# Two 64-column tiles for the last keys' product with V, and a plan with hand-over times per pair of engines

## The chip, the cores and the metric

The kernel runs on one core of one Trainium2 chip. The metric is device time in microseconds (us) of one execution. The engines are PE (TensorE, matrix products), DVE (VectorE), ACT (ScalarE), POOL (GpSimd) and SP, whose queue issues every DMA.

## What is computed

Three stages, one after the other, on 8 batches of 576 rows:

```python
scores = scale * np.matmul(q, k.transpose(0, 1, 3, 2))      # 8 heads, head_dim 64
thresh = np.max(scores, axis=-1, keepdims=True) - tau
scores = np.where(scores >= thresh, scores, -1000000000.0)
attn = softmax(scores); x = attn @ v                        # heads side by side: 512 columns
k = np.maximum(xk @ w_k, 0.0)     # xk, xr mix a row with the one before it
v = k * k @ w_v                   # 512 -> 1024 -> 512
x = sigmoid(xr @ w_r) * v
gate = sigmoid(conv(x))           # causal convolution over rows, 5 taps for each column
out = (gate * (x @ w_val)) @ w_out
```

All inputs are float32 (the weights float64). Attention's product with V is done in fp32. The scores and the five weight products are done as sums of three fp32r products of split operands: high with high, high with low, low with high.

## The kernel before, in words

Attention goes over 32 pairs of heads. A pair is cut into 9 chunks of 128 query rows by 576 keys: four for one head, four for the other, and a last one that holds the 64 left-over rows of both. For each chunk PE makes the scores (L524; L534 for the first pair), DVE takes the minimum (L549), ACT the exponential (L562), POOL adds the threshold (L552), DVE masks and sums (L571), POOL normalizes (L584). Then the probabilities are turned on PE: in the first four pairs straight from `p` in fp32 (L610), after that from a copy `pr` that a DMA makes (L638), in fp32r (L608). ACT brings the result back (L621, L624; the last 64 keys in L629, L632).

Twice a pair follows the product with V, once for 256 columns of query rows and once for 320. The two heads write the two halves of one PSUM bank: for each of four groups of 128 keys, L674 multiplies V of one head into partitions 0 to 63 and V of the other into 64 to 127, each as a column tile of 128 rows by 64 columns of the array. The last 64 keys of both heads come in one product over all 128 rows and 128 columns (L677): `v[:, 512:640]` holds V of head one in its upper left quarter, V of head two in its lower right quarter and zeros elsewhere. As operands are fp32, each product is two matmul instructions in the trace: 16 of L674 and 2 of L677 for each of the 64 products with V.

The first gated layer (names `xk`, `k`, `kh`, `vo`; products with `w_k` and `w_v` at L751) runs in blocks of 512 rows and is woven into the attention of later batches, since a block needs whole rows of x. The tail, after attention, holds the last products with `w_v` and then, block by block, the products with `w_r` (`r`), `w_val` (`val`) and `w_out` (`out`), 36 of each, 12 matmuls a product, all at L751. Between them DVE mixes rows for r (L810), multiplies y = gate times v (L1023), does the convolution's four later taps (L1067, in place in PSUM, two instructions a tap where a block spans two batches) and multiplies gate with val (L1090).

The order of everything is set at build time. Each step is an `Op` with an engine, a duration, what it waits for, a priority and the buffers that it takes and gives back. `Plan.order` is a list scheduler: it plays the program through with these durations and lets each free engine take the ready step of lowest priority number. What it finds is the fixed order of instructions on each engine; on the chip an engine then waits for semaphores in that order. Some steps may go to either of two engines (the low halves on DVE or POOL, the squares on ACT or POOL), and the plan decides. Of waits it knew one number: a step that depends on another engine is ready `HOP` ns after the other ends, a DMA's reader `DMA_MARGIN` later still:

```python
push(end + hop, "free", pick)
x.ready = max(x.ready, end + pick.lat + (DMA_MARGIN if e == "dma" else 0.0) + (SAME.get(e, 0.0) if x.eng == e else hop))
```

The keys (`EARLY`, `W_KEY`, `MIX2`, `CONV_LAG`, `OUT_LAG` and others) shift the priorities of kinds of steps against each other.

Of the kernel before, what the change touches and what calls it, by code (L numbers as in the profile page):

```python
# [63 lines left out]

class Op:
    __slots__ = ("eng", "dur", "lat", "fn", "prio", "acq", "rel", "after", "left", "ready", "start", "idx", "got",
                 "port", "mode")


class Plan:  # L70
# [7 lines left out]
        self.ops = []  # L78
        self.tokens = {}

    def op(self, eng, dur, fn, deps=(), prio=0.0, acq=(), rel=(), lat=0.0, port=False, mode=0):
        o = Op()
        o.port, o.mode = port, mode
        o.eng, o.dur, o.lat, o.fn, o.prio, o.acq, o.rel = eng, dur, lat, fn, prio, acq, rel
        o.start = None
        o.after, o.ready, o.idx = [], 0.0, len(self.ops)
        o.left, o.got = 0, []
        for d in deps:
            if d is not None:
                d.after.append(o)  # L90
                o.left += 1
        self.ops.append(o)
        return o

    def order(self, hop):


        free = dict(self.tokens)
        since = {}
# [3 lines left out]
        n = 0  # L103
        port, mode = 0.0, 0
# [13 lines left out]
        while events:  # L118
            now = events[0][0]
            while events and events[0][0] <= now:  # L120
                _, _, kind, o = heapq.heappop(events)
# [7 lines left out]
                            since[x] = now  # L129
            for e in ENGINES:  # L130
                while busy[e] <= now and ready[e]:
                    skipped, pick, held = [], None, None
                    while ready[e]:
                        x = heapq.heappop(ready[e])
                        if x[2].start is not None:
                            continue
                        if held is not None and x[0] > held[0] + PORT_SLACK:
                            skipped.append(x)
                            break
                        if all(any(free[a] > 0 for a in t) if isinstance(t, tuple) else free[t] > 0  # L140
                               for t in x[2].acq):
                            if e == "dve" and x[2].port and port > now + PORT_TOL:
                                if held is None:
                                    held = x
                                    continue
                            else:
                                pick = x[2]
                                break
                        skipped.append(x)
                    if held is not None:  # L150
                        if pick is None:
                            pick = held[2]
                        else:
                            skipped.append(held)
                    if e == "pe" and mode == 1 and pick is not None and pick.mode != 1:
                        late = pick.prio + GANG
                        while ready[e]:
                            x = heapq.heappop(ready[e])
                            if x[2].mode == 1 and x[0] <= late and all(free[t] > 0 for t in x[2].acq):
# [9 lines left out]
                        break  # L169
                    for t in pick.acq:  # L170
                        if isinstance(t, tuple):
                            t = min((a for a in t if free[a] > 0), key=lambda a: since.get(a, 0.0))
# [7 lines left out]
                    if e == "pool" or e == "dve" and pick.port:  # L180
                        hold = pick.dur
# [21 lines left out]
                    end = now + pick.dur  # L203
                    busy[e] = end
                    push(end, "idle", pick)
                    push(end + hop, "free", pick)
                    for x in pick.after:
                        x.ready = max(x.ready, end + pick.lat + (DMA_MARGIN if e == "dma" else 0.0) + (SAME.get(e, 0.0) if x.eng == e else hop))
                        x.left -= 1
                        if not x.left:  # L210
                            push(x.ready, "ready", x)
# [2 lines left out]

EARLY, QK_EARLY, T_LATE, EV_EARLY, AV_LATE = 166.8448, 0.7689, -0.6136, 186.5584, 0.3905
S3_CHUNKS = 40
MOE_LAG = 0.5912
MOE_STEP = 0.8255  # L220
KSTAGE = 3

LATE_PAIRS = 6
# [5 lines left out]
CVB = 3  # L229
GATES = {"a": 1, "b": 3}  # L230
XRS = {"a": 1, "b": 1}
MIX_EARLY, SIDE_EARLY = -36.7205, 2.0832
W_KEY, W_STEP = -0.8604, 71.1806
V_KEY, V_STEP = 38.9587, 2.2987
EXP_EARLY, MASK_EARLY, SUM_EARLY, NORM_EARLY, MOVE_EARLY, PREP_EARLY, XE_EARLY, KH_EARLY, KL_EARLY = -3.4426, 0.0367, 0.3513, 0.4532, 3.8756, 0.7807, 10.363, 1.0147, -4.2659
MORE_KEYS = ("EXP_EARLY", "MASK_EARLY", "SUM_EARLY", "NORM_EARLY", "MOVE_EARLY", "PREP_EARLY", "XE_EARLY", "KH_EARLY", "KL_EARLY")
R_AHEAD = 0
HOP, DMA_MARGIN, MARGIN = 269.8939, 482.1964, 1.011
VAL_LAG, OUT_LAG = 1.6991, 2.9796
LATE2, LOAD2, MIX2, CONV_LAG, THR_EARLY = 79.2985, -22.1186, -62.0727, 28409.2718, 280.5553  # L240
MIX_AT = 12.996
OUT_FETCH = 1039.5206

PORT_TOL, PORT_SLACK = 839.1264, 3.4377
WARM = 3400.0
SWITCH = 200.0
GANG = 5.9257
# [4 lines left out]
ENGINES = ("dma", "pe", "dve", "act", "pool", "none")  # L252


@with_exitstack
def body(ctx, tc, qka, qkb, vp, w_k, w_v, w_r, w_val, w_out, conv_w, par, out):
# [243 lines left out]
    def chunk(g):  # L500
# [163 lines left out]
        if c in (3, 8):  # L664
# [3 lines left out]
            def av():  # L668
                pt, ptl = pt_t[pi, half]
                v = v_t[pi]  # L670
                acc = av_t[pi, half] = bank(av_op[pi, half])
                for kc in range(4):
                    for h in range(2):
                        nc.tensor.matmul(acc[h * 64:h * 64 + 64, 0:n],  # L674
                                         lhsT=v[:, kc * 128 + h * 64:kc * 128 + h * 64 + 64],
                                         rhs=pt[:, h, kc, 0:n], start=(kc == 0), stop=False)
                nc.tensor.matmul(acc[:, 0:n], lhsT=v[:, 512:640], rhs=ptl[:, 0:n], start=False, stop=True)  # L677

            def evac_x():
                if half == 0:  # L680
# [181 lines left out]
    def moe1(n, at):  # L862
# [32 lines left out]
            l = f["lo"] = op(K_LO, 0, lo, (h,), pr - KL_EARLY, rel=("k2",), port=True)  # L895
            kparts.append((h, l))
        if n < NM - 1:
            mix_k(n + 1, at + MIX_AT * u)
# [284 lines left out]
```

## Time and profile before

| what | value |
|---|---|
| median of 3 runs | 1214.2 us (1214.2 to 1215.7) |
| span of the profiled execution | 1214.2 us |
| PE busy | 1181.0 us (97%) |
| DVE busy | 881.2 us (73%) |
| ACT busy | 859.7 us (71%) |
| POOL busy | 718.5 us (59%) |
| mean granted clock of TensorE | 0.998 |

The profiled execution took as long as the median, so no step between the two is needed. PE's busy time counts overlapping matmuls once, and it counts time in which an instruction has begun but its weights are not in place; a stretch that reads as 100% busy can still hold dead time. Where this matters, the distance from one instruction's start to the next is the better number.

### The profile page before, as it was taken

The page shows a single profiled execution, that of the slowest core. Times are in us where ns is not written, and L with a number is a line of the kernel's source. Part 1 is how long each engine was busy: PE and PEld are TensorE (multiplying, and loading weights), DVE is VectorE, ACT ScalarE, POOL GpSimd, SP SyncE. Part 2 cuts the span into 40 slices and gives each one's busy share as a digit, 9 for nine tenths or more (in the row PEclk, how much of TensorE's full clock was granted, in tenths as well). Part 3 has the DMA queues.
Part 4 walks back from the last instruction along what each step waited for, and adds up shares of the span by engine and source line. Part 5 has one row for each costly group of instructions (what it writes and reads, how often), then busy time and mean ns, then how long its engine had stood idle before and what let it go on. Part 6 is the DMA issues. An engine that isn't in the chain of part 4 may idle for free.

```text
span 1214.2 us, 20512 instructions
## 1 busy us (share of the span) xinstructions
PE 1181.0 (97%) x6798; PEld 948.9 (78%) x6798; DVE 881.2 (73%) x1998; ACT 859.7 (71%) x1637; POOL 718.5 (59%) x960
## 2 busy tenths in 40 slices
PE   6888999999999999999999999999999999999998
PEld 4666788878888778878788778878887877888887
DVE  7999988888888788888877767732314997666650
ACT  7998977898788678778868857745536677654432
POOL 5887776688668668667765766531205755444321
PEclk9999999999999999999999999999999999999999
DMA  6445655567655675556555455325204333221111
GB/s 224 148 160 191 220 189 216 204 234 282 228 183 199 228 243 208 191 209 228 218 209 210 171 186 182 148 86 192 70 23 186 120 124 105 94 82 59 61 52 70
DMA packets 70777, 201.38 MB, mean 166 GB/s; under 512 B 8720, under 2 KB 21136, under 8 KB 68752
## 3 DMA queue, kind: packets, MB, share of 16 engines
q1 hardware_dynamic: 70672, 200.08, 45.9%
q8 instruction: 54, 0.88, 0.3%
q14 instruction: 51, 0.42, 0.1%
HBM read 91.07 MB, written 34.67 MB: 104 GB/s over the span
## 4 chain that ended last, share of the span: by engine, by line
PE 75%; DVE 7%; DMA 3%; POOL 2%; issue 2%; ACT 1%; SPq 0%; DVEq 0%; POOLq 0%; ACTq 0%
PE g L751 47%; PE s L524 11%; PE g L674 8%; PE g L608 6%; DVE g L1067 3%; PE g L677 3%; DMA pr<-p 2%; DVE y L1023 1%; DVE xf L810 1%; DMA stage<-in_w_val 1%; DVE gate L1090 1%; DMA raw<-in_qka 1%; DVE sm L549 0%; ACT p L562 0%; POOL xrl L832 0%
## 5 line engine op out<-in xcount | busy, mean ns | idle before, releaser
L549 DVE TENSOR_REDUCE sm<-s 128x1 f32<-128x576 f32 x288 | 214.3, 751 | 71.9 <-PE s L524 63.9
L571 DVE SCALAR_TENSOR_TENSOR p<-s,sm,p 128x576 f32<-128x576 f32 x288 | 231.2, 812 | 42.0 <-ACT p L562 22.0
L562 ACT ACTIVATE p<-s,sm 128x576 f32<-128x576 f32 x288 | 212.4, 749 | 43.2 <-DVE sm L549 23.5
L584 POOL TENSOR_SCALAR p<-p,sm 128x576 f32<-128x576 f32 x234 | 188.4, 809 | 81.5 <-DVE sm L581 68.6
L524 PE MATMUL s<-qkh 128*128 128x288 f32 x620 | 194.7, 330 | 5.2 <-DVE p L571 5.0
L524 PE MATMUL s<-kl,qkh 128*128 128x288 f32 x620 | 173.6, 296 | 1.2 <-DVE kl L462 1.2
L621 ACT ACTIVATE pt<-g 128x512 f32<-128x512 f32 x256 | 145.4, 603 | 33.6 <-PE g L608 31.2
L552 POOL TENSOR_SCALAR sm<-sm,gs 128x1 f32<-128x1 f32 x288 | 109.2, 381 | 87.0 <-DVE sm L549 62.9
L674 PE MATMUL g<-pt,v 128*64 128x320 f32 (+1 forms) x1024 | 138.8, 413 | 0.9 <-ACT pt L624 0.8
L524 PEld LDWEIGHTS s<-qkh 128*128 128x128 f32 x620 | 116.8, 188 | 17.2 <-DVE p L571 4.9
L608 PEld LDWEIGHTS g<-ident_r,pr 128*128 128x128 f32 (+1 forms) x1148 | 118.9, 140 | 14.5 <-ACT p L562 2.0
L608 PE MATMUL g<-ident_r,pr 128*128 128x128 f32 (+1 forms) x1148 | 123.4, 242 | 5.9 <-ACT p L562 1.4
L1067 DVE SCALAR_TENSOR_TENSOR g<-y,cw_t,g 128x128 f32<-128x128 f32 (+25 forms) x256 | 125.0, 517 | 4.2
L524 PEld LDWEIGHTS s<-kl,qkh 128*128 128x128 f32 x620 | 117.2, 189 | 8.4 <-DVE kl L462 1.4
L751 PE MATMUL g<-xkh,w_k_hi 128*128 128x512 f32 x288 | 116.4, 404 | 0.1
L751 PE MATMUL g<-kh,w_v_hi 128*128 128x512 f32 x288 | 115.5, 401 | 0.0
L751 PE MATMUL g<-xkh,w_k_lo 128*128 128x512 f32 x288 | 112.8, 392 | 0.0
L751 PE MATMUL g<-kh,w_v_lo 128*128 128x512 f32 x288 | 112.6, 391 | 0.0
L674 PEld LDWEIGHTS g<-pt,v 128*64 128x64 f32 x1024 | 68.1, 137 | 55.7 <-issue 9.3
L468 POOL TENSOR_TENSOR qkh<-raw,qkh 64x576 fp32r<-64x576 f32 x62 | 90.1, 1454 | 15.7 <-ACT qkh L458 7.0
L832 POOL TENSOR_TENSOR xrl<-xf,xrh 128x512 fp32r<-128x512 f32 x36 | 48.3, 1351 | 76.2 <-ACT xrh L829 76.0
L1032 POOL TENSOR_TENSOR yl<-y,yh 128x512 fp32r<-128x512 f32 x36 | 48.5, 1358 | 74.6 <-ACT yh L1029 74.6
(112 smaller groups left out, 2561.4 us busy)
## 6 DMA issues: line engine op xcount, KB each, us to landing
pr<-p SPq DMA_DIRECT2D x112, 576.0 KB, 3.5
raw<-in_qkb SPq DMA_DIRECT2D x31, 640.0 KB, 4.5
raw<-in_qka SPq DMA_DIRECT2D x31, 608.0 KB, 4.6
v<-in_vp SPq DMA_DIRECT2D x32, 320.0 KB, 3.3
x_d<-x SPq DMA_DIRECT2D x32, 290.0 KB, 4.1
v_d<-vo SPq DMA_DIRECT2D x36, 256.0 KB, 2.5
vt<-v_d SPq DMA_DIRECT2D x9, 1024.0 KB, 4.8
pr<-p SPq DMA_DIRECT2D x28, 288.0 KB, 2.8
```

The source lines that it names most:

```text
L468: nc.gpsimd.tensor_tensor(out=t["hi"][lo_rows, qs], in0=t["raw"][lo_rows, qs], in1=t["hi"][lo_rows, qs].bitcast(F32), op=ALU.subtract)
L524: nc.tensor.matmul(s_t[g][:, hh, 0:NT], lhsT=q, rhs=k, start=(i == 0), stop=(i == len(terms) - 1))
L549: nc.vector.tensor_reduce(out=sm[:, 0:1], in_=s_t[g][:, :, 0:NT], op=ALU.min, axis=AX.XY)
L552: nc.gpsimd.tensor_scalar(out=sm_t[g][:, 1:2], in0=sm_t[g][:, 0:1], scalar1=tau_t, scalar2=1.0, op0=ALU.add, op1=ALU.mult)
L562: nc.scalar.activation(out=view(), in_=s_t[g][:, :, 0:NT], func=AF.Exp, bias=sm_t[g][:, 0:1], scale=-1.0)
L571: nc.vector.scalar_tensor_tensor(out=view(), in0=s_t[g][:, :, 0:NT], scalar=sm[:, 1:2], in1=view(), op0=ALU.is_le, op1=ALU.mult, accum_out=to)
L584: nc.gpsimd.tensor_scalar(out=view(), in0=view(), scalar1=sm_t[g][:, 3:4], scalar2=1.0, op0=ALU.mult, op1=ALU.mult)
L608: nc.tensor.transpose(o_.bitcast(F32R), in_=i_.bitcast(F32R), identity=ident_r)
L621: nc.scalar.activation(out=pt[:, head, :, q0:q0 + 128], in_=ps.rearrange("p (k q) -> p k q", k=4), func=AF.Copy)
L674: nc.tensor.matmul(acc[h * 64:h * 64 + 64, 0:n], lhsT=v[:, kc * 128 + h * 64:kc * 128 + h * 64 + 64], rhs=pt[:, h, kc, 0:n], start=(kc == ...
L751: nc.tensor.matmul(ps()[:, 0:tw], lhsT=W[w][wt][:, kc, m * 128:(m + 1) * 128].bitcast(F32R), rhs=a(at, kc), start=(i == 0 and x == 0), sto ...
L1067: nc.vector.scalar_tensor_tensor(out=f["ps"][:, x:at + w], in0=t["y"][:, c, x + k:at + w + k], scalar=cw[:, c, k:k + 1], in1=f["ps"][:, x: ...
```

## The change

The product of the last keys with V is cut into the same two column tiles as the other four groups of keys. The two zero quarters of `v[:, 512:640]` are still multiplied.

```diff
-                nc.tensor.matmul(acc[:, 0:n], lhsT=v[:, 512:640], rhs=ptl[:, 0:n], start=False, stop=True)
+                for h in (0, 64):
+                    nc.tensor.matmul(acc[h:h + 64, 0:n], lhsT=v[:, 512 + h:576 + h], rhs=ptl[:, 0:n], start=False, stop=True)
-            o = av_op[pi, half] = op("pe", (3000 if half else 2430) * slow, av, deps, lt + AV_LATE, acq=(BANKS,),
+            o = av_op[pi, half] = op("pe", 2930 if half else 2390, av, deps, lt + AV_LATE, acq=(BANKS,),
```

The plan's single hand-over time becomes a table by pair of engines, with a time of its own for giving back a buffer, and a factor on two durations goes:

```diff
+        def reach(e, f, hop):
+            if isinstance(f, dict):
+                return hop + max(HOPS[e][g] for g in f)
+            return SAME.get(e, 0.0) if e == f else hop + HOPS[e][f]
-                    push(end + hop, "free", pick)
+                    push(end + hop + FREE[e], "free", pick)
-                        x.ready = max(x.ready, end + pick.lat + (DMA_MARGIN if e == "dma" else 0.0) + (SAME.get(e, 0.0) if x.eng == e else hop))
+                        x.ready = max(x.ready, end + pick.lat + (DMA_MARGIN if e == "dma" else 0.0) + reach(e, x.eng, hop))
-HOP, DMA_MARGIN, MARGIN = 269.8939, 482.1964, 1.011
+HOP, DMA_MARGIN, MARGIN = 30.0, 480.0, 1.011
+HOPS = {"pe": dict(pe=0, act=200, dve=200, pool=200, dma=200, none=200),
+        "dve": dict(pe=170, act=110, dve=130, pool=175, dma=150, none=170),
...
+FREE = dict(pe=200, dve=170, act=200, pool=120, dma=100, none=0)
-        slow = 1.02
+        slow = 1.0
```

All keys of the plan get other values, of which two lines stand here for all. An operand `hold` is also added, which can keep a buffer for a step that waits; no step sets it.

```diff
-LATE2, LOAD2, MIX2, CONV_LAG, THR_EARLY = 79.2985, -22.1186, -62.0727, 28409.2718, 280.5553
+LATE2, LOAD2, MIX2, CONV_LAG, THR_EARLY = 42.4429, -35.4801, -230.8294, 12594.8319, 251.622
```

With that the order on every engine is another one. In PE's order, one product with V of 320 columns (the twentieth of the 64) stood like this before; `s` are scores, `g` a bank of PSUM:

```order
L524 MATMUL s<-qkh 128x288
L524 MATMUL s<-kl,qkh 128x288
L674 MATMUL g_3242<-pt,v 64x320 x8
L677 MATMUL g_3242<-ptl,v 128x320
L524 MATMUL s<-qkh 128x288
L524 MATMUL s<-kl,qkh 128x288
```

Now its counterpart is:

```order
L539 MATMUL s<-qkh 128x288
L539 MATMUL s<-kl,qkh 128x288
L689 MATMUL g_3278<-pt,v 64x320 x8
L693 MATMUL g_3278<-ptl,v 64x320 x2
L539 MATMUL s<-qkh 128x288
L539 MATMUL s<-kl,qkh 128x288
```

The full-width product of the last keys has become two half-width ones; the neighbours are of the same kind. The first full-width instruction behind the eight column tiles is now one of fp32r scores.

In the tail, DVE's order before went on like this after the eighth product of gate and val (`xf` is the mix for r, the rows with `cw_t` are taps):

```order
L1090 TENSOR_TENSOR gate<-g_11751,gate 128x512
L1023 TENSOR_TENSOR y<-gate,vt 128x512
L810 SCALAR_TENSOR_TENSOR xf<-xt,par_t,g_11886 128x256
L1023 TENSOR_TENSOR y<-gate,vt 128x512
L810 SCALAR_TENSOR_TENSOR xf<-xt,par_t,g_11886 128x256
L1067 SCALAR_TENSOR_TENSOR g_11798<-y,cw_t,g_11798 128x128
L1067 SCALAR_TENSOR_TENSOR g_11798<-y,cw_t,g_11798 128x380
L1067 SCALAR_TENSOR_TENSOR g_11865<-y,cw_t,g_11865 128x128
```

Now, at the same place:

```order
L1106 TENSOR_TENSOR gate<-g_11952,gate 128x512
L826 SCALAR_TENSOR_TENSOR xf<-xt,par_t,g_11977 128x192
L1039 TENSOR_TENSOR y<-gate,vt 128x512
L826 SCALAR_TENSOR_TENSOR xf<-xt,par_t,g_12004 128x320
L1039 TENSOR_TENSOR y<-gate,vt 128x512
L826 SCALAR_TENSOR_TENSOR xf<-xt,par_t,g_12004 128x192
L1039 TENSOR_TENSOR y<-gate,vt 128x512
L1083 SCALAR_TENSOR_TENSOR g_11904<-y,cw_t,g_11904 128x128
```

The mixes for later blocks' r have moved forward. Between the eighth and the ninth product of gate and val DVE now has 43 instructions (11 mixes, 4 of y, 28 taps), where it had 28 (4, 4 and 20). On PE, 19 products with `w_r` and 8 with `w_val` now stand ahead of the first with `w_out`, where it was 12 and 8; after that a round of four each goes three `r`, one `out`, one `r`, two `out`, one `val`, one `out`, three `val`, where before `out` and `r` alternated one by one and four `val` followed.

## Rows read from the trace of the kernel before

**Rows 1.** The page's head: span, and busy time of each engine.
```profile
span 1214.2 us, 20512 instructions
PE 1181.0 (97%) x6798; PEld 948.9 (78%) x6798; DVE 881.2 (73%) x1998; ACT 859.7 (71%) x1637; POOL 718.5 (59%) x960
```
**Rows 2.** Engines by stretch: length, then busy us (instructions) of PE, PEld, DVE, ACT, POOL.
```profile
0.00:20.00 20.00, 12.31 (x58) 6.74 (x60) 11.96 (x27) 13.32 (x26) 8.71 (x20) 1.00 0.73 257
60.00:105.00 45.00, 38.68 (x264) 28.40 (x262) 42.73 (x84) 40.98 (x82) 38.94 (x56) 0.96 0.51 178
150.00:300.00 150.00, 150.00 (x987) 121.59 (x987) 125.10 (x323) 122.04 (x239) 113.41 (x167) 1.00 0.61 223
920.00:1020.00 100.00, 97.37 (x424) 78.69 (x423) 91.55 (x177) 72.83 (x140) 66.52 (x53) 1.00 0.39 138
```
**Rows 3.** PE's waits from 150 to 820: total us, times, longest.
```profile
PE g L608 <- DMA pr<-p: 1.2, 1, 1.2
PE g L608 <- ACT vo L907: 1.1, 1, 1.1
PE g L608 <- ACT x L684: 0.9, 1, 0.9
PE s L524 <- DVE p L571: 0.8, 2, 0.5
```
**Rows 4.** Chain of work around two products with V: start, us, what.
```profile
245.07 2.30 PE g L674 x16
247.38 0.74 PE g L677 x2
...
257.49 1.88 PE g L674 x16
259.37 0.63 PE g L677 x2
```
**Rows 5.** PE in order of time around the same: start, us, line, tile, count.
```profile
257.20 0.29 PE L524 MATMUL s<-kl,qkh 128*128 128x288 f32 x1
257.42 1.95 PE L674 MATMUL g<-pt,v 128*64 128x256 f32 x16
259.30 0.70 PE L677 MATMUL g<-ptl,v 128*128 128x256 f32 x2
...
260.07 0.39 PE L751 MATMUL g<-xkh,w_k_lo 128*128 128x512 f32 x1
```
**Rows 6.** Chain: thirteen fp32r transposes of 128 columns in a row.
```profile
624.68 1.08 PE g L608 x13
```
**Rows 7.** PE's instructions by line, 150 to 820: the last keys' product.
```profile
L677 PE MATMUL g<-ptl,v 128*128 128x256 f32 (+1 forms) x104 | 39.1, 458 | 0.0
```
**Rows 8.** ACT by line, 20 to 110: two rows, the shortest and longest kinds used.
```profile
L454 ACT ACTIVATE qkh<-raw,gs 128x640 fp32r<-128x640 f32 (+1 forms) x9 | 7.5, 831 | 0.0
L684 ACT ACTIVATE x<-g 128x256 f32<-128x256 f32 (+1 forms) x9 | 3.9, 429 | 0.2 <-PE g L677 0.2
```
**Rows 9.** Two lines by themselves: durations min/median/max ns, first and last start.
```profile
L1023 DVE TENSOR_TENSOR y<-gate,vt x36: 682/691/1792, 922.4 to 1156.3; 128x512 f32<-128x512 f32 x36
L751 PE MATMUL g<-kl,w_v_hi x288: 387/389/475, 168.0 to 913.8; 128*128 128x512 f32 x144
```
**Rows 10.** DVE by line, 922.3 to 1022.1: busy us, mean ns, idle before.
```profile
L1067 DVE SCALAR_TENSOR_TENSOR g<-y,cw_t,g 128x128 f32<-128x128 f32 (+7 forms) x112 | 55.5, 521 | 1.7
L1023 DVE TENSOR_TENSOR y<-gate,vt 128x512 f32<-128x512 f32 x18 | 19.1, 1077 | 0.8 <-PE g L751 0.8
L810 DVE SCALAR_TENSOR_TENSOR xf<-xt,par_t,g 128x192 f32<-128x192 f32 (+4 forms) x36 | 17.0, 474 | 5.6 <-ACT g L799 4.2 <-POOL xrl L832 1.4
L1090 DVE TENSOR_TENSOR gate<-g,gate 128x512 f32<-128x512 f32 x12 | 8.1, 682 | 0.0
```
**Rows 11.** The chain's end.
```profile
1022.02 187.99 PE g L751 x828
...
1210.04 0.60 ACT o L1115
```
**Rows 12.** Chain: two of the copies that transposes waited for.
```profile
410.87 5.41 DMA pr<-p
...
711.19 7.54 DMA pr<-p
```
**Rows 13.** The page's DMA issues: KB each, median us from issue to landing.
```profile
pr<-p SPq DMA_DIRECT2D x112, 576.0 KB, 3.5
```

More of the change, by code (lines that the diff above doesn't have):

```diff
@@ L66 @@
     __slots__ = ("eng", "dur", "lat", "fn", "prio", "acq", "rel", "after", "left", "ready", "start", "idx", "got",
-                 "port", "mode")
+                 "port", "mode", "hold")
 class Plan:
@@ L79, in __init__, with op @@
         self.tokens = {}
-    def op(self, eng, dur, fn, deps=(), prio=0.0, acq=(), rel=(), lat=0.0, port=False, mode=0):
+    def op(self, eng, dur, fn, deps=(), prio=0.0, acq=(), rel=(), lat=0.0, port=False, mode=0, hold=()):
         o = Op()
-        o.port, o.mode = port, mode
+        o.port, o.mode, o.hold = port, mode, hold
         o.eng, o.dur, o.lat, o.fn, o.prio, o.acq, o.rel = eng, dur, lat, fn, prio, acq, rel
@@ L131, in order @@
                 while busy[e] <= now and ready[e]:
-                    skipped, pick, held = [], None, None
+                    skipped, pick, held, kept = [], None, None, ()
                     while ready[e]:
@@ L139, in order @@
                             break
-                        if all(any(free[a] > 0 for a in t) if isinstance(t, tuple) else free[t] > 0
-                               for t in x[2].acq):
+                        if all(any(free[a] > 0 and a not in kept for a in t) if isinstance(t, tuple)
+                               else free[t] > 0 and t not in kept for t in x[2].acq):
                             if e == "dve" and x[2].port and port > now + PORT_TOL:
@@ L148, in order @@
                                 break
+                        elif x[2].hold and free["x"] > 0:
+                            kept = x[2].hold
                         skipped.append(x)
@@ L158, in order @@
                             x = heapq.heappop(ready[e])
-                            if x[2].mode == 1 and x[0] <= late and all(free[t] > 0 for t in x[2].acq):
+                            if x[2].mode == 1 and x[0] <= late and all(free[t] > 0 and t not in kept for t in x[2].acq):
                                 skipped.append((pick.prio, pick.idx, pick))
@@ L171, in order @@
                         if isinstance(t, tuple):
-                            t = min((a for a in t if free[a] > 0), key=lambda a: since.get(a, 0.0))
+                            t = min((a for a in t if free[a] > 0 and a not in kept), key=lambda a: since.get(a, 0.0))
                             pick.got.append(t)
@@ L213, in order @@
         return out
-EARLY, QK_EARLY, T_LATE, EV_EARLY, AV_LATE = 166.8448, 0.7689, -0.6136, 186.5584, 0.3905
+EARLY, QK_EARLY, T_LATE, EV_EARLY, AV_LATE = 75.1647, 1.8278, -2.0346, 153.7854, 1.5185
 S3_CHUNKS = 40
 MOE_LAG = 0.5912
-MOE_STEP = 0.8255
+MOE_STEP = 0.7879
 KSTAGE = 3
@@ L231 @@
 XRS = {"a": 1, "b": 1}
[L232 to L235, printed above, removed]
+MIX_EARLY, SIDE_EARLY = -34.628, 2.644
+W_KEY, W_STEP = -1.5423, 25.8964
+V_KEY, V_STEP = 20.9718, 6.154
+EXP_EARLY, MASK_EARLY, SUM_EARLY, NORM_EARLY, MOVE_EARLY, PREP_EARLY, XE_EARLY, KH_EARLY, KL_EARLY = -2.5135, 0.0304, 0.3776, 0.5121, 2.3441, 2.7971, 2.9697, 1.433, 0.072
 MORE_KEYS = ("EXP_EARLY", "MASK_EARLY", "SUM_EARLY", "NORM_EARLY", "MOVE_EARLY", "PREP_EARLY", "XE_EARLY", "KH_EARLY", "KL_EARLY")
 R_AHEAD = 0
-HOP, DMA_MARGIN, MARGIN = 269.8939, 482.1964, 1.011
-VAL_LAG, OUT_LAG = 1.6991, 2.9796
-LATE2, LOAD2, MIX2, CONV_LAG, THR_EARLY = 79.2985, -22.1186, -62.0727, 28409.2718, 280.5553
-MIX_AT = 12.996
-OUT_FETCH = 1039.5206
-PORT_TOL, PORT_SLACK = 839.1264, 3.4377
+HOP, DMA_MARGIN, MARGIN = 30.0, 480.0, 1.011
+VAL_LAG, OUT_LAG = 2.4158, 4.2372
+LATE2, LOAD2, MIX2, CONV_LAG, THR_EARLY = 42.4429, -35.4801, -230.8294, 12594.8319, 251.622
+MIX_AT = 1.1188
+OUT_FETCH = 1042.669
+PORT_TOL, PORT_SLACK = 842.0121, 3.4087
 WARM = 3400.0
 SWITCH = 200.0
-GANG = 5.9257
+GANG = 2.2937
 RAW_TO = 1
@@ L252 @@
 ENGINES = ("dma", "pe", "dve", "act", "pool", "none")
+HOPS = {"pe": dict(pe=0, act=200, dve=200, pool=200, dma=200, none=200),
+        "dve": dict(pe=170, act=110, dve=130, pool=175, dma=150, none=170),
+        "act": dict(pe=200, act=0, dve=195, pool=185, dma=150, none=200),
+        "pool": dict(pe=120, act=60, dve=50, pool=0, dma=100, none=120),
+        "dma": dict(pe=0, act=0, dve=0, pool=0, dma=0, none=0),
+        "none": dict(pe=0, act=0, dve=0, pool=0, dma=0, none=0)}
+FREE = dict(pe=200, dve=170, act=200, pool=120, dma=100, none=0)
 @with_exitstack
@@ L897, in moe1 @@
         if n < NM - 1:
-            mix_k(n + 1, at + MIX_AT * u)
+            mix_k(n + 1, at + MIX_AT)
         for m in range(KD):
```

## Prediction

> **What bounds the kernel now.** I read the page's head first: PE is busy 97% of the span, the other engines 59 to 73% [rows 1]. The stretches show where the missing time sits. From 150 to 300 us PE has no idle time at all [rows 2], and from 150 to 820 its named waits come to 4.0 us in five waits, none over 1.2 us [rows 3]. Before 150 us it is different: in 60 to 105 us PE lacks 6.3 of 45 us while DVE is busy 42.7 and ACT 41.0 [rows 2]; the softmax and the splitting of weights set the pace there. In the tail PE lacks 2.6 us between 920 and 1020 while DVE is busy 91.6 of 100 [rows 2], and DVE's own rows between 922.3 and 1022.1 add up to 99.7 us of work in 99.8 us [rows 10]. After 1022.0 the chain is 828 matmuls of `L751` without a break, 188.0 us or 0.227 us each, then one eviction at 1210.0 [rows 11]. So the end is set by PE's work, plus what PE loses in the first 150 us, plus what it loses until DVE lets go at 1022.
>
> **The product of the last keys.** 64 more columns make sixteen column-tile matmuls 2.30 instead of 1.88 us long [rows 4]. They run in eight pairs, so a pair costs 0.42/8 = 0.0525 us per 64 columns, 0.21 us for 256. Eight pairs are 1.68 of 1.88 us: 0.20 us is not columns. The two full-width matmuls take 0.63 us for 256 columns and 0.74 for 320 [rows 4], of which 2 x 0.21 and 2 x 0.2625 are columns: 0.21 us is dead, in both. The order in time splits the dead time [rows 5]. The last score starts at 257.20, needs 0.13 and is followed at 257.42: 0.09 us. From 259.30, the first of `L677`, to 260.07, the second of `L751`, are 0.77 us, of which 0.42 and 0.227 are columns: 0.12 us, the wait for the first 128 fp32 weights. The rest of the 0.21, again about 0.09, lies before `L677` starts. Each change between the half and the full width thus costs about 0.09, and the fp32 weights behind it 0.12.
>
> After the change the last keys are one more round like the four before: four matmuls in two pairs, 2 x 0.21 us, as much as the two full-width ones took in columns. The change of width is still there, but now the instruction behind it is an fp32r one. Thirteen fp32r transposes in a row take 1.08 us, 0.083 each [rows 6]; 128 columns in one pass are 0.21/4 = 0.053, so a load of 128 fp32r weights shows at most 0.03 us. The saving is 0.12 - 0.03 = 0.09 us a product if 0.09 for the width stays. Its ends are 0 (all dead time moves to the next instruction) and 0.21 (all goes). Of the 128 `L677` matmuls 104 stand where PE is never short of work [rows 7], so 52 of the 64 products count: 52 x 0.09 = 4.7 us, ends 0 and 10.9. I take 4.7, by the transposes, the nearest full-width fp32r rows.
>
> Two rules of the Trainium skill bear on this. "TensorE: Matmul & The Clock Gate", section "Weight-path perf modes", has 128 weights that are not FP32 load faster than FP32 ones; rows 6 against the 0.12 us of rows 5 agree, and the sum by it is the one above. "TensorEngine Tiling (Array Packing)", section "Key Properties", says that changing the tiling mode drains TensorE; the 0.09 us on both sides of rows 5 agree, and by that rule alone nothing is saved, since the change of mode only moves behind the new pairs.
>
> **The start.** Counted in the order, ten ACT instructions fewer stand ahead of the first product with `w_k` (two exponentials, two casts of keys and queries, pieces of weights and others). At 0.43 to 0.83 us each [rows 8] that is about 6.7 us. But at the 84th matmul of that layer the instructions ahead of it on ACT are again as many: 158.8 us of work now, 159.3 before, each kind at its mean duration. The head start is spent before PE has stopped waiting for ACT, and I count 0, with ends of -6.7 (it is all kept) and +2 (the same work with two more waits of the size of rows 3).
>
> **The middle.** All of it is moved, and none of PE's work is added or taken but that of the first part. PE idles 4.0 us there [rows 3]; the ends are -4.0 and +4.0, and I take 0, since PE's queue of ready work is what covers the moves. Without that cover each late copy would cost about 1.2 us [rows 3].
>
> **The tail.** PE's work behind the last product with `w_v` (913.8 us, rows 9) is the same: 1284 matmuls, 291.5 us. What differs is how much DVE must have done ahead of a given place. Before, the binding place is 456 matmuls in: DVE starts y at 922.4 [rows 9] and gives the last of 18 y, 36 mixes, 112 taps and 12 gate products at 1022.0; 828 matmuls remain, 188.0 us. Now the worst place by the order is 661 matmuls in, behind 27 y, 50 mixes, 176 taps and 16 gate products. With rows 10 (0.496 a tap, 0.472 a mix, 0.675 a gate product, 19.1 for the first 18 y) and the median 0.691 for 9 further y [rows 9] that is 87.3 + 23.6 + 10.8 + 25.3 = 147.0 us: DVE is there at 1069.4, 623 matmuls or 141.4 us remain, and PE ends at 1210.8, where it was 1210.0. If the 8.1 us of idle time in rows 10 does not recur in the added work, the 47.3 added us shrink by the same share to 43.5, PE ends at 1207.0 by this place, and DVE is no longer what ends last. With every y at the 1.06 us of the first 18, it would be 3.3 later. So -3.0 to +4.1; I take 0, between the two nearest results.
>
> **Sum.** 1214.2 - 4.7 + 0 + 0 + 0 = 1209.5 us, against a span and a median that are both 1214.2.
>
> **The rivals.**
> *The width's price only moves (no change).* The exit from half width, weights included, costs the next instruction the same 0.21 us. For it: the price of the width is there on both sides in rows 5, and rows 6 show fp32r weights only where the width does not change. Against it: the 0.12 us of rows 5 belong to fp32 weights. Then the sum is 1214.2, with +-2 from the new order. By the skill's rule on draining this is the result.
> *More is saved.* Both parts of the 0.21 us go, for instance because the next weights are in place by then: 52 x 0.21 = 10.9, hence 1203.3. Nothing in the rows shows weights of the full width loaded under column tiles.
> *DVE binds later in the tail (slower).* Moving the mixes for r forward puts 43 instead of 28 DVE instructions between the eighth and the ninth gate product, ahead of taps that products with `w_out` wait for. With 4.7 us saved before, y begins at 917.7; the time is 917.7 plus DVE's work W ahead of the 661st matmul, plus 141.4 of PE and the 4.2 us from PE's end to the span's: 1063.3 + W. From W = 151 this is later than before. If each y takes 1.06 us (3.3 more) and idle time recurs as in rows 10 on top (8.1 in 100, so 3.8 on 47), W is 154.1 and the time 1217.4. For it: DVE has no slack at all in rows 10. Against it: the y behind the first 18 are short, as the median of 0.691 in rows 9 says.
> *The copies come too late.* A DMA's reader was planned 752 ns after the landing time (270 + 482), now 510 (30 + 480). The copy `pr` lands 3.5 us after issue in the median [rows 13], but 5.4 and 7.5 us at 411 and 711 us [rows 12], where weights are moved. Eight more late copies at 1.2 us [rows 3] are 9.6 us: 1219. Against it: with 1.45 us for the transfer and 1.7 behind it the plan still allows 3.66 us, before 3.90, and the median lies under both.
> *The change does not do what it says:* the new half-width matmuls run one by one. That would be 64 x 0.42 us more, at most 27 us; the sixteen before them run in pairs [rows 4], so I give it no chance of its own.
>
> **Chances and range.** Forecast (0.05 to 0.12 us a product saved, the rest within 2.5 us of nothing): 0.50, of which 0.42 faster and 0.08 within 0.2%. Price only moves: 0.20 (0.03 faster, 0.13 the same, 0.04 slower). More saved: 0.12, faster. DVE later: 0.13, slower. Copies: 0.05, slower. 0.2% is 2.4 us, about what a measurement here can tell from no change. Together faster 0.57, the same 0.21, slower 0.22. The forecast's own range is 1206 to 1213; to hold 8 in 10 it has to reach the middle of both sides, 1203.5 to 1216.5.
>
> **What would show it.** Right: 256 matmuls at the new line, the step from its first to the second full-width instruction behind shorter than 0.77 us by about 0.1 where a product with `w_k` follows; PE without idle time from 150 to 820 but for some 4 us; the last unbroken run of products starting between 1017 and 1066 us. Wrong: full-width instructions behind the new line that start as late as before (the price moved); DVE named before PE's waits between 1020 and 1070; more than three waits for `pr` copies after 150 us.

## The result: 0.9% slower, outside the range

| | before | changed |
|---|---|---|
| median | 1214.6 us (1213.4 to 1215.7, 6 runs) | 1225.8 us (1220.2 to 1227.5, 6 runs) |
| ratio | | 1.0086 [1.0066, 1.0106] |
| span of the profiled execution | 1214.2 us | 1218.4 us, and 1.8 around it |

I had forecast 1209.5 us and a range of 1203.5 to 1216.5. The profiled execution of the changed kernel is the quickest of its six, 5.6 us under its median; so where its profile shows 4 us, the median holds 11. Each profiled execution on record after the forecast took 1.8 us longer than its span. If that holds for the profile of before (span 1214.2), its execution took about 1216.0, 1.4 over the median; I had taken that span and that median for the same. The profile of the second experiment, which keeps the new order and has a span of 1225.7 us, stands in below for the usual execution.

**The page's head and the stretches.** Head of the page of the changed kernel:

```profile
span 1218.4 us, 20782 instructions
PE 1179.8 (97%) x6926; PEld 942.4 (77%) x6926; DVE 879.2 (72%) x1992; ACT 854.9 (70%) x1631; POOL 735.6 (60%) x972
```

Stretches of the same trace (length, then busy time and instructions of PE, PEld, DVE, ACT, POOL, the granted clock, DMA share, GB/s):

```profile
60.00:105.00 45.00, 37.13 (x267) 28.74 (x269) 44.16 (x87) 41.41 (x82) 38.68 (x59) 0.96 0.47 160
150.00:300.00 150.00, 148.41 (x996) 118.09 (x995) 129.67 (x322) 119.84 (x235) 112.67 (x162) 1.00 0.59 215
920.00:1020.00 100.00, 97.49 (x426) 79.30 (x425) 90.30 (x174) 78.66 (x155) 72.17 (x58) 1.00 0.45 158
```

PE is busy 1.2 us less than before [rows 1], and the span is 4.2 longer. The 128 more matmuls are the split product; they did not lengthen PE's busy time. Between 60 and 105 us it is busy 37.1 instead of 38.7 of 45. From 150 to 300 us, where PE had no idle time [rows 2], 1.6 us are missing. Between 920 and 1020 us PE's share is what it was.

**The split, in PE's order of time.** The same product with V as in [rows 5] (start, us, line, tile, count):

```profile
256.31 0.29 PE L539 MATMUL s<-kl,qkh 128*128 128x288 f32 x1
256.53 1.95 PE L689 MATMUL g<-pt,v 128*64 128x256 f32 x16
258.31 0.60 PE L693 MATMUL g<-ptl,v 128*64 128x256 f32 x4
258.84 0.50 PE L767 MATMUL g<-xkh,w_k_hi 128*128 128x512 f32 x1
259.18 0.40 PE L767 MATMUL g<-xkh,w_k_lo 128*128 128x512 f32 x1
```

From the first column tile to the second full-width product with `w_k` it is 259.18 - 256.53 = 2.65 us. Before, it was 260.07 - 257.42 = 2.65 us [rows 5]. Nothing is saved. It is the same elsewhere: with scores behind, this step from the first column tile to the second full-width instruction has a median of 2.55 us for 256 columns and 3.08 for 320, in the kernel before and in the first experiment below, which has the old order and the new product. Only the four products with 128-column transposes behind them got shorter, by 0.05 us each. The four new matmuls take their 0.42 us of columns, to 258.73. The first full-width instruction starts 0.11 later, at 258.84, and the next 0.34 behind that, of which 0.227 are columns: again 0.11. These 0.22 us are as much as the 0.21 that stood around `L677`.

**PE's waits from 150 to 820** (total us, times, longest), first the changed kernel:

```profile
PE s L539 <- DVE p L586: 2.4, 5, 0.8
PE g L623 <- ACT x L700: 1.8, 3, 0.8
PE g L623 <- ACT k L892: 1.1, 1, 1.1
PE g L623 <- ACT qkh L473: 0.8, 1, 0.8
PE g L623 <- DMA pr<-p: 0.5, 1, 0.5
```

and the new order with the old product (second experiment), its two longest rows:

```profile
PE g L623 <- ACT x L699: 3.0, 4, 1.2
PE s L539 <- DVE p L586: 3.0, 4, 1.1
```

Before they came to 4.0 us in five waits [rows 3]; now 6.6 in eleven, and in the second experiment 9.7 in sixteen. Hardly any of it is put down to a copy. Who is late shows one step further back, on ACT. These are the exponential's waits for a copy over the whole span, of before, of the changed kernel and of the second experiment:

```profile
ACT p L562 <- DMA pr<-p: 5.5, 3, 2.9
```

```profile
ACT p L577 <- DMA pr<-p: 11.7, 10, 2.3
```

```profile
ACT p L577 <- DMA pr<-p: 16.5, 10, 2.6
```

The exponential does not read `pr`. It writes a new `p`, and needs a buffer that the copy out of an older `p` gives back only when it has landed. Behind the exponential DVE's masking waits, in the changed kernel and in the second experiment:

```profile
DVE p L586 <- ACT p L577: 30.9, 46, 3.2
```

```profile
DVE p L586 <- ACT p L577: 37.3, 47, 3.5
```

where in the kernel before it was

```profile
DVE p L571 <- ACT p L562: 22.0, 35, 2.9
```

and behind the masking wait PE's scores, whose bank of PSUM DVE still reads.

**The chain's end**, in the changed kernel (start, us, what):

```profile
1059.20 0.78 DVE y L1039
1059.97 0.48 DVE g L1083
...
1060.48 0.43 DVE g L1083
1060.93 0.60 ACT gate L1088
...
1061.58 152.63 PE g L767 x672
...
1214.23 0.60 ACT o L1131
```

DVE lets go at 1060.9 with 672 matmuls left; before it was 1022.0 with 828 left [rows 11]. From the first y (its line by itself: durations, first and last start)

```profile
L1039 DVE TENSOR_TENSOR y<-gate,vt x36: 680/809/1797, 925.0 to 1130.5; 128x512 f32<-128x512 f32 x36
```

to PE's end it is 1214.2 - 925.0 = 289.2 us, where it was 1210.0 - 922.4 = 287.6 [rows 9, 11]: the tail is 1.6 us longer, and starts 2.6 later. In the second experiment, the usual execution, it starts at 931.2, 8.8 later than before, and takes 290.2 us.

### The profile page after: what moved, and what is told of

The parts are those of the page before. It is cut to its first block, busy times and chain, and to the rows that moved or that the text cites. A ratio compares the mean times of both kernels' runs of the same rounds, so it can differ in the third digit from the quotient of the medians.

```text
span 1218.4 us, 20782 instructions
## 1 busy us (share of the span) xinstructions
PE 1179.8 (97%) x6926; PEld 942.4 (77%) x6926; DVE 879.2 (72%) x1992; ACT 854.9 (70%) x1631; POOL 735.6 (60%) x972
## 4 chain that ended last, share of the span: by engine, by line
PE 45%; DVE 8%; DMA 3%; ACT 2%; issue 1%; POOL 0%; SPq 0%; DVEq 0%; ACTq 0%; POOLq 0%
PE g L767 32%; PE s L539 5%; DVE g L1083 4%; PE g L689 4%; PE g L623 3%; DVE y L1039 2%; DVE xf L826 1%; DMA xt<-x_d 1%; PE g L693 1%; DMA vt<-v_d 1%; DMA pr<-p 1%; DVE gate L1106 1%; ACT g L815 0%; ACT xrh L845 0%; DMA v_d<-vo 0%
## 5 line engine op out<-in xcount | busy, mean ns | idle before, releaser
L564 DVE TENSOR_REDUCE sm<-s 128x1 f32<-128x576 f32 x288 | 211.8, 751 | 66.0 <-PE s L539 57.9
L577 ACT ACTIVATE p<-s,sm 128x576 f32<-128x576 f32 x288 | 209.8, 749 | 61.0 <-DVE sm L564 37.3
L599 POOL TENSOR_SCALAR p<-p,sm 128x576 f32<-128x576 f32 x234 | 191.2, 822 | 72.5 <-DVE sm L596 46.5
L539 PE MATMUL s<-qkh 128*128 128x288 f32 x620 | 189.2, 322 | 5.9 <-DVE p L586 5.6
L636 ACT ACTIVATE pt<-g 128x512 f32<-128x512 f32 x256 | 141.2, 602 | 26.0 <-PE g L623 23.3
L623 PEld LDWEIGHTS g<-ident_r,pr 128*128 128x128 f32 (+1 forms) x1148 | 113.6, 140 | 20.6 <-ACT p L577 2.7
L1083 DVE SCALAR_TENSOR_TENSOR g<-y,cw_t,g 128x64 f32<-128x64 f32 (+28 forms) x256 | 124.5, 518 | 4.5 <-ACT g L1078 0.3
L623 PE MATMUL g<-ident_r,pr 128*128 128x128 f32 (+1 forms) x1148 | 118.8, 245 | 7.2 <-DMA pr<-p 3.2
L1115 POOL TENSOR_TENSOR gvl<-gate,gvh 128x512 fp32r<-128x512 f32 x36 | 47.6, 1324 | 95.7 <-PE g L767 48.4
```

The source lines that it names most:

```text
L539: nc.tensor.matmul(s_t[g][:, hh, 0:NT], lhsT=q, rhs=k, start=(i == 0), stop=(i == len(terms) - 1))
L564: nc.vector.tensor_reduce(out=sm[:, 0:1], in_=s_t[g][:, :, 0:NT], op=ALU.min, axis=AX.XY)
L577: nc.scalar.activation(out=view(), in_=s_t[g][:, :, 0:NT], func=AF.Exp, bias=sm_t[g][:, 0:1], scale=-1.0)
L599: nc.gpsimd.tensor_scalar(out=view(), in0=view(), scalar1=sm_t[g][:, 3:4], scalar2=1.0, op0=ALU.mult, op1=ALU.mult)
L623: nc.tensor.transpose(o_.bitcast(F32R), in_=i_.bitcast(F32R), identity=ident_r)
L636: nc.scalar.activation(out=pt[:, head, :, q0:q0 + 128], in_=ps.rearrange("p (k q) -> p k q", k=4), func=AF.Copy)
```

## The experiments

The theories: *split* (the product saves or costs), *copies* (buffers `p` come back too late in the new plan) and *tail* (DVE binds later).

**1 and 2. Each half alone.** The first puts the split product into the kernel before, with its own plan:

```diff
-                nc.tensor.matmul(acc[:, 0:n], lhsT=v[:, 512:640], rhs=ptl[:, 0:n], start=False, stop=True)
+                for h in (0, 64):
+                    nc.tensor.matmul(acc[h:h + 64, 0:n], lhsT=v[:, 512 + h:576 + h], rhs=ptl[:, 0:n], start=False, stop=True)
```

> The kernel before, with the last keys' product cut into two column tiles and nothing else; the plan still counts the old durations, so every engine's order is that of before. Theory A (the price of the change of width only moves to the instruction behind the new pairs, as the 309 ns step behind the new line in the changed kernel's trace says): the same as before within 1.5 us. Rival B (0.09 us saved on each of the 52 products in the saturated stretch): 4.7 us faster. Rival C (the two half-width matmuls hurt somewhere the profile does not name): 3 us or more slower.

Measured: 1213.9 us (1212.4 to 1216.7, 11 runs), 0.9992 [0.9983, 1.0002] of before.

The second puts the full-width product back into the changed kernel (the diff above, reversed).

> The changed kernel's plan and order, with the full-width product of the last keys put back. Theory A (all of the loss is the new order): as slow as the changed kernel, about 11 us over before, with runs spread over several us as there. Rival C (the split is what costs): within 2 us of before.

Measured: 1227.1 us, 1.0100 [1.0085, 1.0115]. The split is worth nothing that these runs can show, and the new order is all of the loss.

**3 and 4. The two halves of the plan.** The third is the changed kernel with the key values of the one before; the fourth keeps the new keys and has a single hand-over time (the third's edit sets the key lines alone and is not shown):

```diff
-HOP, DMA_MARGIN, MARGIN = 30.0, 480.0, 1.011
+HOP, DMA_MARGIN, MARGIN = 269.8939, 482.1964, 1.011
...
+HOPS = {e: {f: 0.0 for f in ENGINES} for e in ENGINES}
+FREE = {e: 0.0 for e in ENGINES}
```

> The changed kernel with all keys of before; the table of hand-over times (and HOP 30, DMA margin 480) stays. If shorter hand-over times by themselves make an order that leaves too little time for real waits: at least 5 us slower than before. If the keys are what costs: within 3 us of before.

Measured: 1234.1 us, 1.0157 [1.0139, 1.0175].

> The changed kernel with its new keys, but one hand-over time of 269.9 ns for every pair and 482 for DMA, as before. If the keys are what costs: about 11 us slower than before. If the table is what costs: within 3 us of before. If the keys fit only the table they were set for: slower than the changed kernel itself.

Measured: 1235.4 us, 1.0163 [1.0141, 1.0185]. Each of the two is slower than both halves together, so the loss can't be shared out between them by time.

The third is also not a clean half. One more line of the change, not shown so far, sets the place of the mix for the next block:

```diff
-            mix_k(n + 1, at + MIX_AT * u)
+            mix_k(n + 1, at + MIX_AT)
```

`u` is `MOE_STEP / 64`, 0.013. So the old `MIX_AT` of 12.996 sets the priority number of that mix 0.17 above `at` in the kernel before and 13.0 above in the third. What this does to the third's time no run separates, so its time says nothing certain of the table by itself. The fourth is not touched by this.

The waits for copies do differ. The exponential's, with the new table and the old values of the keys:

```profile
ACT p L578 <- DMA pr<-p: 11.4, 12, 3.1
```

and with the new keys and the one old time:

```profile
ACT p L572 <- DMA pr<-p: 2.8, 3, 1.6
```

They are long in the changed kernel, the second and the third, which have the table, and short in the fourth, which has not. So they fit the table; with the line above in the third, that is not proved. What else makes these two slow is in part their start. In the third, PE is short of work between 150 and 198 us, and in the second of these stretches its granted clock averages 0.75, that is, part of the stretch is at 1.2 instead of 2.4 GHz (columns as above):

```profile
150.00:171.00 21.00, 18.98 (x138) 15.43 (x134) 19.73 (x54) 19.09 (x39) 18.91 (x28) 1.00 0.67 256
171.00:198.40 27.40, 22.73 (x134) 17.52 (x133) 21.47 (x56) 20.51 (x41) 22.07 (x33) 0.75 0.57 194
```

The kernel before has 183 matmuls in the second of these stretches, against 134. The fourth has 160 there, of 24.5 us busy.

**5 and 6. Copies of a few rows.** From the third copied pair on, a copy moves 16 of its 128 rows; all steps and waits stay. The other rows of `pr`, and so the attention, are left out. Five is the changed kernel, six the one before with the same edit.

```diff
-            nc.sync.dma_start(out=pr_t[pi, j][:, 0:w], in_=p_t[pi, j][:, 0:w])
+            r = 128 if pi < COPY_FROM + 2 else 16
+            nc.sync.dma_start(out=pr_t[pi, j][0:r, 0:w], in_=p_t[pi, j][0:r, 0:w])
```

> The changed kernel in its own order, but from the seventh pair on each copy of probabilities (pr<-p) moves 16 of 128 rows; it leaves out 7/8 of that data, so the attention of those pairs is computed from old probabilities. Theory D (the exponentials wait for buffer p, which the copy gives back later than the plan counts, and PE waits behind them and sometimes falls to half clock): ACT's waits for pr<-p, 11.7 to 16.5 us in the changed order, fall below 3 us, and the time falls by 5 to 9 us, to 1217 to 1221, with a spread as small as that of before. Rival E (many small waits of other kinds; the copies are only one of them): 1223 to 1226.

Measured: 1213.3 us, 0.9990 [0.9977, 1.0002].

> The kernel before with the same short copies (the same 7/8 of the data left out), as the control. Theory D: its ACT waits for pr<-p were 5.5 us in three places, so at most 2 to 3 us faster than before, 1211.5 to 1214.5. Rival F (shorter transfers help any order by themselves): it gains as much as the changed order does.

Measured: 1210.2 us, 0.9967 [0.9955, 0.9978]. Both are quicker than I had expected. The DMA rows of five (count, KB each, median us from issue to landing):

```profile
raw<-in_qkb SPq DMA_DIRECT2D x31, 640.0 KB, 4.0
raw<-in_qka SPq DMA_DIRECT2D x31, 608.0 KB, 4.3
pr<-p SPq DMA_DIRECT2D x104, 72.0 KB, 2.5
```

The copies land in 2.5 instead of 3.6 us and the loads of `raw` take as long as in the changed kernel (4.1 and 4.3); those of `v` and the stores of `x` became quicker (3.4 each, from 3.8 and 3.9). That these others account for the gain does not fit the waits: of all that the engines of the changed kernel wait for a DMA between 150 and 820 us, 14.1 us, 12.2 are for the copies, and of 19.6 in the second experiment 17.1. So it is the copies that act. Against the kernel before, the changed order goes from 11.2 us slower to 1.7 under it (level, given the interval), a gain of 12.9; the old order gains 4.8. The difference, 8.1 us, is what late copies cost the new order more than the old one. The exponential's waits fall to 3.7 us in five. A short copy helps both who wait for it, the exponential that needs `p` back and the transposes that read `pr`; this pair of runs does not separate them.

**7 and 9. Three taps.** The convolution's first later tap is left out: a quarter of DVE's taps, nothing of PE's work. Seven is the changed kernel, nine the one before.

```diff
-                for b, s0, w, at in parts_of:
+                for b, s0, w, at in parts_of if k else ():
```

> The changed kernel in its own order, with the convolution's earliest tap left out (64 of 256 DVE instructions of the tail, some 31 us of DVE's work; the convolution then has four taps instead of five). If DVE sets the tail until 1061 us: products run without a break from about 922 us, the stretch from the last score to the last product shrinks from 392.6 to 388 us, and the time by 4 to 5 us, to about 1221. If something else (the fetches of xt or vt) holds the tail: less than 1.5 us.

Measured: 1218.9 us, 1.0032 [1.0018, 1.0045].

> The kernel before in its own order with the convolution's earliest tap left out (four taps of five), as the control of the changed kernel without it, which became 7.0 us faster. If the changed tail loses more to DVE than the old one did: the gain here is smaller by the 1.6 to 2.7 us by which the tails differ, so 4 to 5.5 us, 1209.5 to 1211. If both tails hang on DVE alike: 7 us, 1208.

Measured: 1211.7 us, 0.9975 [0.9965, 0.9985]. The gain is 11.2 - 3.9 = 7.3 us in the new order and 3.0 in the old, a difference of 4.3 that belongs to DVE in the new tail. With DVE out of the way the chain of seven ends in one unbroken run of products, and nearly the whole tail is PE:

```profile
826.89 103.60 PE g L767 x456
933.40 280.70 PE g L767 x1237
```

The profiles of these runs show that the two losses lie in two places (us; the tail is from the first y to PE's last product):

| | first y starts | tail |
|---|---|---|
| old order: before | 922.4 | 287.6 |
| old order, split product (1) | 921.1 | 287.7 |
| old order, short copies (6) | 917.2 | 287.0 |
| old order, three taps (9) | 923.5 | 284.0 |
| new order: changed, its quickest execution | 925.0 | 289.2 |
| new order, old product (2) | 931.2 | 290.2 |
| new order, short copies (5) | 917.9 | 289.4 |
| new order, three taps (7) | 930.9 | 283.2 |

Short copies bring the first y of the new order back to within 0.7 us of the old one's and leave the tail as it is; a tap less leaves the first y and takes 6.0 to 7.0 us out of the new tail, 3.6 out of the old. By the medians, 8.1 and 4.3 make 12.4 for a loss of 11.2; by their intervals each of the two is known to about 3 us. The profiles show 1.6 to 2.6 for the tail. So the copies have the larger part, some 8 to 9, the tail 2 to 4.

**8. A buffer given back at landing.** The plan waits for the landing latency (its 1.7 us) before it hands a DMA's buffer on:

```diff
-                    push(end + hop + FREE[e], "free", pick)
+                    push(end + hop + FREE[e] + (pick.lat if e == "dma" else 0.0), "free", pick)
```

> The changed kernel, whose plan counts a buffer that a DMA gives back as free only when the data have landed (transfer, latency and hand-over), as it already does for a DMA's readers; keys as in the change, so the order is another one. Theory D: ACT's waits for pr<-p fall below 4 us and the time to 1215 to 1222. Rival G (any order that the keys were not set for is some 20 us slower than before, as with the table alone and the keys alone): 1230 to 1236.

Measured: 1220.3 us, 1.0047 [1.0030, 1.0064], 5.4 over before where the changed kernel is 11.2 over, with keys that were not set for it. It is another order again, so this is not the price of one line of the plan. ACT's wait went where it should, and part of it came back on PE. ACT's row and PE's longest:

```profile
ACT p L577 <- DMA pr<-p: 1.7, 2, 1.0
```

```profile
PE g L623 <- DMA pr<-p: 4.2, 7, 1.3
```

PE's own waits for copies were 0.5 us in one. Why its readers are now early was not separated from the rest of the new order.

**10. With the tail's keys of before** on top (`VAL_LAG`, `OUT_LAG`, `LATE2`, `LOAD2`, `MIX2`, `CONV_LAG`, `OUT_FETCH`).

```diff
...
-LATE2, LOAD2, MIX2, CONV_LAG, THR_EARLY = 42.4429, -35.4801, -230.8294, 12594.8319, 251.622
+LATE2, LOAD2, MIX2, CONV_LAG, THR_EARLY = 79.2985, -22.1186, -62.0727, 28409.2718, 251.622
...
```

> The changed kernel whose plan frees a DMA's buffer at landing, with the seven keys of the tail (LATE2, LOAD2, MIX2, CONV_LAG, VAL_LAG, OUT_LAG, OUT_FETCH) of before; the order up to the end of attention is that of the run with landing alone (1220.3). By the order DVE's worst lead over PE in the tail falls from +5.3 to -2.7 us (before: -0.8). If DVE's order in the tail is what its 2 us are lost to: the tail takes 390 to 391 us instead of 393, the time 1217.5 to 1218.5. If not: 1220 as without these keys.

Measured: 1219.6 us, 1.0041 [1.0025, 1.0058], 0.7 better than eight where about 2 were expected. The chain's end is the old one again:

```profile
1026.70 188.01 PE g L767 x828
```

The first y starts at 926.4, so the tail takes 1214.7 - 926.4 = 288.3 us, where it was 1213.9 - 924.4 = 289.5 in eight and 287.6 in before. By the profiles the tail gained 1.2 us. That the median shows less has a reason ahead of the tail. The order is that of eight until past 929 us, yet the first product with `w_k` starts at 109.8 us in this profile, 107.6 in eight's, on a lower granted clock; the first 150 us of eight and of ten (columns as above):

```profile
0.00:150.00 150.00, 127.97 (x854) 95.55 (x854) 134.01 (x259) 132.94 (x258) 119.53 (x176) 0.98 0.55 188
```

```profile
0.00:150.00 150.00, 126.34 (x839) 95.75 (x841) 133.05 (x257) 131.13 (x255) 116.69 (x174) 0.95 0.53 185
```

The six runs of ten part in the same way: three with a mean granted clock of 0.997 or 0.998 took 1217.2 to 1218.5 us, three with 0.994 took 1220.7 to 1221.6. So the median does not decide whether these keys are worth the 2 us.

**11. The same in the plan before:**

```diff
-                    push(end + hop, "free", pick)
+                    push(end + hop + (pick.lat if e == "dma" else 0.0), "free", pick)
```

> The kernel before, whose plan also frees a DMA's buffer only at landing; keys of before. Theory D: the 5.5 us of ACT's waits for pr<-p shrink and with them some of the 4.3 us that short copies saved there, so 1211 to 1215. Rival G (keys fit only the rule they were set for): 1222 or more.

Measured: 1216.7 us, 1.0019 [1.0010, 1.0028]: 2 us slower, which neither theory had. The exponential's wait for copies fell from 5.5 to 2.0 us, and PE's waits from 150 to 820 rose from five to twelve:

```profile
PE s L524 <- DVE p L571: 2.6, 4, 1.0
PE g L608 <- DMA pr<-p: 1.6, 3, 0.7
```

A wait for copies taken out of an order is not by itself time gained; the whole order changes with it.

**12. A later landing of the copies in the plan** (`COPY_NS`, the time behind the transfer), on top of ten, so that the readers come later as well:

```diff
-P_NS, COPY_NS, LOAD_NS = 1450, 1700, 2300
+P_NS, COPY_NS, LOAD_NS = 1450, 2100, 2300
```

> As the run with landing and the old tail keys, and the plan counts 2100 ns instead of 1700 behind a copy's transfer (3.55 us in all; the copies land in 3.5 to 3.6 us). If the copies' time is what the plan still has wrong: 2 to 4 us faster than with 1700, 1213 to 1216, and ACT's waits for pr<-p under 1.5 us. If the rest of the loss lies elsewhere: no better than with 1700.

Measured: 1215.6 us, 1.0009 [0.9998, 1.0019], 4 us better than ten and level with before. PE's wait for copies fell from 3.8 us in six to one:

```profile
PE g L623 <- DMA pr<-p: 1.2, 1, 1.2
```

while ACT's did not go under 1.5 as expected; it rose from 3.0 to 5.0 in seven. So its gain does not come from a shorter wait of ACT for copies. PE's own wait for copies is another link in the rows, but no run tests it by itself. Keys set anew for a plan that counts the landing were not tried. No kernel with all of the work beat the one before clear of noise.

## Why the prediction was wrong, point by point

**The last keys' product: wrong.** The step "0.12 - 0.03 = 0.09 us a product" failed. The 0.03 came from fp32r transposes in a row [rows 6], where the width does not change. Behind the column tiles the first full-width fp32r instructions lose 0.11 and 0.11 us, as the fp32 ones did. The rival that the price only moves was right: 0.00 us are saved, and the 0.21 us stand behind the new pairs. The Trainium skill, "TensorEngine Tiling (Array Packing)", section "Key Properties", states that a change of the tiling mode drains TensorE; the trace agrees, with 0.22 us behind the column tiles. The Trainium skill, "TensorE: Matmul & The Clock Gate", section "Weight-path perf modes", gives a faster load to weights that are not FP32; at this place the trace does not show it, with 0.11 us for the second fp32r instruction where I had read 0.12 for fp32 weights in [rows 5]. Whether that second 0.11 is the weights at all, as I read it in before, no run separates.

**The start: as counted.** The first product with `w_k` starts at 107.3 us, where it was 109.6 in before, and by 150 to 171 us the two are level again (the layer's 121st matmul starts at 170.8, before at 171.2). The head start was spent, as predicted.

**The middle: wrong, and the largest error.** I took 0 with ends of 4 us, since "PE's queue of ready work is what covers the moves". The loss is some 8 us, and with short copies it is gone. I had the right suspect, the copies, and looked at the wrong reader. I checked whether the transposes on PE would find `pr` late, with the plan's allowance for a DMA's reader (752 ns before, 510 now). The buffer's return has an allowance of its own, `HOP` before (270 ns) and `HOP` with `FREE` now (130 ns), and with neither does the plan count the landing. I read these lines in the diff and gave them no term. The wait at that place is ACT's (11.7 and 16.5 us in ten waits, 5.5 in three before), and [rows 3], which are PE's own, show only its last link. That it is this line of the plan which let the waits grow is an argument and not shown by itself: the kernel before did not count the landing either, and counting it made its order 2 us slower (11). The rival's price (eight copies at 1.2 us, 9.6) was near the measured loss by luck: PE's own waits for copies are 0.5 us in one.

**The tail: the rival was right in place, too dear in price.** DVE's rows between the first y and the place that binds now (busy us, mean ns, idle before):

```profile
L1083 DVE SCALAR_TENSOR_TENSOR g<-y,cw_t,g 128x64 f32<-128x64 f32 (+22 forms) x163 | 78.9, 511 | 3.0 <-ACT g L1078 0.3
L1039 DVE TENSOR_TENSOR y<-gate,vt 128x512 f32<-128x512 f32 x26 | 25.8, 1000 | 1.5 <-PE g L767 0.8 <-DMA vt<-v_d 0.7
L826 DVE SCALAR_TENSOR_TENSOR xf<-xt,par_t,g 128x128 f32<-128x128 f32 (+7 forms) x50 | 24.0, 486 | 3.9 <-ACT g L815 1.9 <-ACT xrh L845 1.5 <-POOL xrl L848 0.5
L1106 DVE TENSOR_TENSOR gate<-g,gate 128x512 f32<-128x512 f32 x16 | 11.0, 685 | 0.1
```

The 26 y average 1.00 us; I had the further ones at 0.691 by the median. That part of the rival held. Idle time came again, 8.5 us in 137, where in [rows 10] it was 8.1 in 100. But it does not come on top of the busy times, as the rival counted it: with 8.1 us idle, 99.7 us of busy rows can fit into 99.8 only because instructions overlap, and by [rows 2] DVE is busy 91.6 us of 100. For the same reason "no slack at all" was a wrong reading. The binding place is 612 matmuls in, not 661, since the 672 that follow run without a break. The rival's sum makes the tail 154.1 + 141.4 = 295.5 us, 7.9 more than before; it was 1.6 to 2.6 longer. That is inside the ends of the step (-3.0 to +4.1), and my 0 lay below it.

**Sum.** Forecast: -4.7 (split) + 0 + 0 + 0. Measured: 0 (split), 0 (start), some 8 to 9 (middle), 2 to 4 (tail). Two of the three signs that I named beforehand came in: full-width instructions as late as before, and DVE named before PE's run at 1061. The third, more than three waits for copies after 150 us, was badly put. The ten are ACT's; PE's waits have one there, of 0.5 us. And the kernel before, with three of ACT's and one of PE's, is over that limit too.

## What to carry to other kernels

Where an order is planned ahead, look at every place in the plan at which a DMA's end is used: the reader of what it wrote, and the next writer of what it read, which in these traces waits for the landing too. Counting it is not by itself a gain: the order that follows is another one, and one of them was slower (11). Look for the late step on the engine that takes the buffer, one or two links ahead of the engine that bounds, since the last engine's waits name only the last link. And a price measured beside a change (dead time behind a change of width) belongs to the change until a run moves the change away from the instruction.

## What was not expected of the hardware

A short lack of work on PE can cost more than its length. In the second experiment the exponential waits 2.44 us for a copy at 367.9, and PE idles 0.69 and 1.21 us behind it:

```profile
367.94 0.74 ACT L577 ACTIVATE p<-s,sm 128x576 f32<-128x576 f32 x1 [2.44 <-DMA pr<-p]
...
369.75 0.37 PE L539 MATMUL s<-qkh 128*128 128x288 f32 x1 [0.69 <-DVE p L586]
...
371.71 0.28 PE L623 MATMUL g<-ident_r,pr 128*128 128x128 f32 x1 [1.21 <-ACT k L891]
```

After that the granted clock is at 0.50, 1.2 instead of 2.4 GHz, for 3.4 us (columns as above):

```profile
368.00:372.00 4.00, 2.10 (x16) 1.64 (x15) 3.14 (x7) 4.00 (x7) 2.72 (x3) 1.00 0.01 3
372.20:375.60 3.40, 3.40 (x15) 3.00 (x14) 2.07 (x8) 2.34 (x7) 3.22 (x4) 0.50 0.42 173
375.60:380.00 4.40, 4.40 (x28) 2.74 (x26) 3.29 (x9) 3.56 (x6) 2.77 (x4) 1.00 0.80 250
```

A product with `w_k` takes 0.63 us there, and 0.39 five microseconds earlier, as PE's order of time shows:

```profile
367.55 0.39 PE L766 MATMUL g<-xkh,w_k_lo 128*128 128x512 f32 x1
...
372.96 0.63 PE L766 MATMUL g<-xkh,w_k_lo 128*128 128x512 f32 x1
```

By these rows half the clock over 3.4 us costs 1.7 us on top of the idle time, an estimate. At the same place the changed kernel's profiled execution waits 1.50 us for the copy and 1.14 on PE, and keeps its clock (granted 1.00 from 364 to 376 us). Between the 24th and the 32nd product with V, where this lies, it takes 98.3 us, and the second experiment 101.5; their spans differ by 7.3. This is one of the ways in which the same order can take 1220 us in one execution and 1227 in another; that it is the whole of that spread is not shown.
